# Attention of five batches beside four tiles, x kept in memory between, and the last two tiles' h by seven products

## The chip, the core and the metric

The kernel runs on one core of a Trainium2 chip. TensorE (PE) multiplies matrices into PSUM banks; VectorE (DVE), ScalarE (ACT) and GpSimd (POOL) work on elements; SyncE (SP) issues all DMA transfers from one queue. The metric is the device time of one execution in microseconds, lower is better. Each engine takes its instructions in a fixed order and waits on semaphores for the results of the others.

## The reference

Two parts. Attention on q, k, v of 8 batches, 8 heads, 576 positions, 64 features: scores `q k^T / 8` plus a slope times the distance for each head, masked to the 128 positions that end at the query's own, softmax, times v. Its output, laid out as x of 4608 tokens x 512 features, goes through an MLP:

```python
scores = scale * np.matmul(q, k.transpose(0, 1, 3, 2))
scores = np.where((rel >= 0) & (rel < window), scores + bias[None], -1e9)
attn = softmax(scores)                      # window 128, bias = -slope * |rel|
x = np.matmul(attn, v)                      # as 4608 x 512
h = x @ w_in                                # 512 -> 2048
g = 0.5 * h * (1.0 + erf(h / sqrt(2)))
return g @ w_out                            # 2048 -> 512
```

All inputs and outputs are float32.

## The kernel before

The 4608 tokens are 9 tiles of 512 (tile 0 to 8), which do not match the 8 batches of 576: batch b fills the end of tile b and the start of tile b+1. Products of float32 are made of float16 pairs: each operand is split into a high part (a cast, on ACT or POOL) and a low part, the scaled operand less the high part (`low_part`, L249, on DVE), and three matmuls (high x high, high x low, low x high) add up in PSUM.

A tile of the MLP has two halves. `mlp_in` makes h for one of 16 blocks of 128 features with 12 matmuls of 128x512 (L763); `gelu` takes GELU on ACT (L786), the high part g on POOL (L787) and the low part on DVE. Then `mlp_out` (L809) makes four column blocks of o, each over all 16 blocks of g, 12 matmuls for 4 of these; `put` evicts them (L820 on ACT, L822 on DVE) and sends them out. A tile is a loop of 32 steps: steps 0 to 15 are the blocks of h, steps 16 to 31 a quarter of an o block each.

Attention of a batch is four units of two heads. `scores` (L533) makes them for bands, `biased` (L563, DVE) adds the bias while leaving PSUM, `softmax` takes maxima (L652, DVE) and exponentials (L655, ACT), POOL makes the high weights e_main (L664), `low_weights` the low ones on DVE; SP's transposing DMAs turn e_main to et (L674). `weigh` (L716) multiplies et by v into av, and `leave` writes av as high and low part (L736 and `low_part`) straight into x of the two tiles. `split_qk`, `split_v`, `stat_v` and the scales prepare the next batch's operands.

Tiles 0 and 1 and batches 0 to 2 are placed instruction by instruction by a long string `ORDER`, each name a task that goes one step further. From tile 2 on the code is the loop: beside tile t stand the four units of batch t+1, their scores at the steps `SCORES_AT` and their weighted sums at `WEIGH_AT` of the same tile. The framework puts the resulting instructions on each engine's queue by its own priorities, so the queue's order can differ from the order of the code.

The last two tiles multiply by seven products: a tile is cut in 2x2 blocks, and seven products of half-size blocks of sums of x and of w replace eight. The sums are made on DVE: `sums_of_weights_out` for w_out, `sums_of_weights` for w_in, `sums_of_x` for x (L890 to L940). FAST and FAST_OUT are the first tile whose h and whose out are made that way: 8 and 7. Thus tile 7 makes h by 192 ordinary matmuls and out by 336 of 128x256 (L1098), tile 8 both by 336 of 128x256 (`Seven`, L1011; `seven_all`, `seven_out`). The sums of w_out are made after tile 6's loop and beside tile 7's h, those of w_in beside tile 7's out.

Of the kernel before, what the change touches and what calls it, by code (L numbers as in the profile page):

```python
# [1380 lines left out]
```

## Time and profile before

| | |
|---|---|
| median of 3 runs | 885.36 us (885.20 to 886.47) |
| profiled execution | 885.17 us |
| its span, first to last instruction | 883.4 us |
| PE busy | 871.1 us (99%) |
| DVE busy | 717.3 us (81%) |
| ACT busy | 543.5 us (62%) |
| POOL busy | 197.9 us (22%) |
| granted clock of PE | 1.00 |

The rows below come from that one execution. A group of instructions carries the line of before's code that issues it; `low_part` is a helper, so all low parts share L249 and are told apart by their tiles. A matmul's record is longer than its share of the engine, since matmuls are pipelined: a group's cost on PE is read from start to start.

### The profile page before, as it was taken

The numbers are of one execution on the slowest core, as the hardware profiler recorded it, in microseconds if no ns is written. First come the engines' busy times: TensorE is split into PE (matmuls) and PEld (weight loads), VectorE is DVE, ScalarE is ACT, GpSimd is POOL, SyncE is SP. The second block draws the span as 40 slices with busy tenths as digits, with TensorE's granted clock in tenths as the row PEclk, the third lists the DMA queues.
The fourth block names the chain that finished last, engine by engine and source line by source line (L and its number), as shares of the span: only waits on it lengthen the run. The fifth ranks groups of instructions, "written<-read, shape, count | busy, mean of one in ns | idle before, by whom it ended". The sixth has DMA issues, their size and how long they took to land.

```text
span 883.4 us, 18563 instructions
## 1 busy us (share of the span) xinstructions
PE 871.1 (99%) x7447; PEld 481.5 (55%) x7447; DVE 717.3 (81%) x1385; ACT 543.5 (62%) x1144; POOL 197.9 (22%) x416
## 2 busy tenths in 40 slices
PE   9899999999999999999999999999999999999998
PEld 4644445545454555455455445545545554588887
DVE  7999999999739874888587875888477999998871
ACT  7999969798635662564474454566355357744750
POOL 2100000122015440452125421543054320000000
PEclk9999999999999999999999999999999999999999
DMA  9955666552652236334622454224132230001001
GB/s 308 306 180 207 199 173 138 165 159 56 173 149 55 55 78 185 94 57 85 184 73 55 102 143 134 55 55 108 49 55 56 66 91 1 1 13 37 1 1 48
DMA packets 174598, 91.63 MB, mean 104 GB/s; under 512 B 133680, under 2 KB 156336, under 8 KB 174384
## 3 DMA queue, kind: packets, MB, share of 16 engines
q1 hardware_dynamic: 174512, 90.45, 37.6%
q8 instruction: 58, 0.95, 0.5%
q14 instruction: 28, 0.23, 0.1%
HBM read 46.53 MB, written 9.44 MB: 63 GB/s over the span
## 4 chain that ended last, share of the span: by engine, by line
PE 80%; DVE 11%; ACT 4%; DMA 2%; issue 2%; POOL 0%; SPq 0%; DVEq 0%; ACTq 0%; POOLq 0%
PE h L763 29%; PE o L809 27%; PE av L716 5%; PE sc L533 4%; PE u_out L1098 4%; PE o L806 2%; PE u L1011 2%; PE v L1011 2%; DMA raw<-w_out 1%; DVE s L563 1%; PE z_out L1098 1%; PE y_out L1098 1%; PE v_out L1098 1%; PE x_out L1098 1%; DVE e_main L249 1%
## 5 line engine op out<-in xcount | busy, mean ns | idle before, releaser
L763 PE MATMUL h<-x,wi 128*128 128x512 f16 x1536 | 336.3, 379 | 0.3 <-DVE wi L249 0.2
L763 PEld LDWEIGHTS <-wi 128*128 128x128 f16 x1536 | 148.2, 98 | 178.7 <-DVE wi L249 1.7
L809 PE MATMUL o<-wo,g 128*128 128x512 f16 x864 | 191.7, 379 | 0.0
L809 PEld LDWEIGHTS <-g 128*128 128x128 f16 x1152 | 111.3, 98 | 133.5
L655 ACT ACTIVATE s<-s,nmax 128x192 f32<-128x192 f32 x252 | 111.5, 445 | 36.0 <-DVE nmax L652 35.8
L249 DVE SCALAR_TENSOR_TENSOR e_main<-s,z,e_main 128x192 f16<-128x192 f32 x252 | 119.4, 509 | 11.8 <-POOL e_main L664 11.5
L787 POOL TENSOR_SCALAR g<-g,sg 128x512 f16<-128x512 f32 x96 | 78.8, 829 | 212.9 <-ACT g L786 212.5
L786 ACT ACTIVATE g<-h,gs 128x512 f32<-128x512 f32 x96 | 62.9, 687 | 73.8 <-PE h L763 42.2
L664 POOL TENSOR_SCALAR e_main<-s,z 128x192 f16<-128x192 f32 x180 | 89.8, 518 | 78.6 <-ACT s L655 58.1
L249 DVE SCALAR_TENSOR_TENSOR g<-g,sg,g 128x512 f16<-128x512 f32 x96 | 84.0, 901 | 21.3 <-POOL g L787 21.2
L563 DVE SCALAR_TENSOR_TENSOR s<-sc,cs,bias_h 128x384 f32<-128x384 f32 x112 | 64.3, 609 | 13.5 <-PE sc L533 13.4
L809 PE MATMUL o<-wo_first,g 128*128 128x512 f16 x288 | 66.1, 379 | 0.0
L652 DVE TENSOR_REDUCE nmax<-s 128x5 f32<-128x960 f32 (+1 forms) x56 | 58.1, 1047 | 3.2 <-POOL s L568 2.1
L806 PE MATMUL o<-zo,g 128*128 128x512 f32 x128 | 56.7, 597 | 0.0
L533 PE MATMUL sc<-kbuf,qbuf 64*64 64x192 f16 (+1 forms) x1656 | 53.0, 254 | 3.1 <-DVE s L563 1.8
L568 POOL MEMSET s<- 64x64 f32 (+1 forms) x112 | 19.2, 172 | 158.9 <-DVE s L563 150.7
L736 ACT ACTIVATE x<-av,cx 128x448 f16<-128x448 f32 (+6 forms) x52 | 24.5, 482 | 45.8 <-PE av L716 40.9
L655 ACT ACTIVATION_READ_ACCUMULATOR s<-s,nmax 128x1 f32 x252 | 47.9, 190 | 0.0
L716 PEld LDWEIGHTS <-vbuf 128*64 128x64 f16 x1680 | 40.4, 111 | 8.2 <-issue 6.7
L533 PEld LDWEIGHTS <-qbuf 64*64 64x64 f16 x1512 | 34.3, 106 | 18.4 <-issue 17.5
L716 PE MATMUL av<-et,vbuf 128*64 128x128 f16 (+1 forms) x1680 | 42.7, 210 | 0.3 <-DVE s L563 0.3
L820 ACT ACTIVATE ob<-o,so 128x512 f32<-128x512 f32 x12 | 8.2, 682 | 54.3 <-PE o L809 54.3
(270 smaller groups left out, 1147.3 us busy)
## 6 DMA issues: line engine op xcount, KB each, us to landing
v<-vp SPq DMA_DIRECT2D x32, 320.0 KB, 5.6
out<-ob SPq DMA_DIRECT2D x34, 256.0 KB, 2.3
raw<-w_in SPq DMA_DIRECT2D x8, 1024.0 KB, 11.7
raw<-w_out SPq DMA_DIRECT2D x8, 1024.0 KB, 5.1
q<-qp SPq DMA_DIRECT2D x7, 1152.0 KB, 6.3
k<-kp SPq DMA_DIRECT2D x7, 1152.0 KB, 6.0
qbuf<-qp SPq DMA_DIRECT2D x4, 288.0 KB, 6.1
kbuf<-kp SPq DMA_DIRECT2D x4, 288.0 KB, 5.2
```

The costliest lines, as they stand in the source:

```text
L249: return nc.vector.scalar_tensor_tensor(out=dst, in0=src, scalar=scale, in1=high, op0=ALU.mult, op1=ALU.subtract)
L533: done = nc.tensor.matmul(ps[bank][o, n, 0:W], a, m, start=(i == 0), stop=(i == len(terms) - 1 and b > 0), skip_group_check=True,)
L563: yield nc.vector.scalar_tensor_tensor(out=s[:, bank[0] : bank[0] + k, :], in0=ps[bank][:, 0:k, 0:W], scalar=cs, in1=bias.broadcast_to([P, ...
L655: yield nc.scalar.activation(s[:, i, :], s[:, i, :], AF.Exp, bias=nmax[:, i : i + 1], accum_out=z[:, i : i + 1])
L664: yield nc.gpsimd.tensor_scalar(e[:, i, 0, c], s[:, i], z[:, i : i + 1], 1.0, op0=ALU.mult, op1=ALU.mult)
L716: done = nc.tensor.matmul(av[r, (j - blocks[0]) * QB : (j - blocks[0] + len(js)) * QB], v32s[b][:, hp, kb, r] if b < EXACT else vbuf[:, vi ...
L763: done = nc.tensor.matmul(ph, wi[n][:, a, cc, k * P : (k + 1) * P], x[:, cc, b, :], start=(i == 0), stop=(i == 3 * NCC - 1),)
L786: yield nc.scalar.activation(g32, ph, AF.Gelu, scale=gsc[t, n])
L787: yield nc.gpsimd.tensor_scalar(g[:, r, 0], g32, gsg[t, n], 1.0, op0=ALU.mult, op1=ALU.mult)
L806: done = nc.tensor.matmul(o, g[:, r, c], zo[n][:, n % 2, k * DM : (k + 1) * DM], start=(fc == first), stop=(fc == last))
L809: done = nc.tensor.matmul(o, g[:, r, a, c], wo[n][:, b, k, :], start=(fc == first and i == 0), stop=(fc == last and i == 2),)
L1098: nc.tensor.matmul(ps[name][:, tb], f(d, a)[:, k, tb * P : (tb + 1) * P], w(d, b, k), start=first, stop=True, skip_group_check=True,)
```

## The change

FAST becomes 7, so that tile 7 makes its h by seven products too. For that the sums of w_out and w_in and of tile 7's x must be there when tile 7 starts. Attention of batches 3 to 7 is no longer bound to the tile beside it: its 20 units are placed by two tables over the 128 steps of tiles 2 to 5 (step 0 is the first of tile 2), five batches beside four tiles, and tile 6 has none, but the sums of weights. `split_v(3)` goes into the early string. Since x of a later tile is then ready long before its tile, and there is room for two x only, `leave` writes pieces of x of tiles 4 to 8 into a stage of four slots, SP sends each to memory (36 writes), and `load_x` brings a tile's x back (5 loads of 1 MB). The early string, the PSUM banks and the turns of the buffers are new tables.

```diff
-FAST = 8
+FAST = 7
+LOAD_AT = 29
+SCORES_AT = (2, 8, 14, 19, 29, 34, 40, 44, 53, 59, 65, 69, 79, 84, 90, 94, 104, 110, 115, 118)
+WEIGH_AT = (16, 21, 26, 26, 42, 45, 48, 52, 65, 71, 74, 79, 90, 97, 97, 102, 115, 121, 126, 126)
+SPLIT_AT, STAT_AT, SUMS_AT = (1, 1, 1, 1), (8, 10, 9, 8, 10), (26, 28, 35, 38)
+STAGED = 4
+ATTEND = 5
 FAST_OUT = 7
 HT = TT // 2
 NTILE = NT // TT
...
-z0 z0 b b z0 s0 m00 s0 x00 m00 z1 m00 z1 x00 b F s0 z2 x00 x00 m01 x00 m01 n00 n00 n00 x01 z1 b z2 x01 s1 x01 x01 a0
...
+z0 z0 b b z0 b s0 z1 z1 m00 m00 x00 x00 s0 z1 F x00 m00 b z2 s0 x00 m01 x00 m01 x01 x01 s1 n00 x01 x01 n00 n00 s1 a0
...
+    memory = ctx.enter_context(tc.tile_pool(name="x_all", bufs=1, space=bass.MemoryType.DRAM))
...
+    stage, staged = [], {}
     def x_tile(t):
         if t not in xt:
+            if t >= STAGED:
+                turn_of["x"] = stage[1]
             xt[t] = room([P, NCC, 2, TT], F16, "x", f"x{t}", 2)
         return xt[t]
+    def x_in_memory(t):
+        if t not in staged:
+            staged[t] = memory.tile([P, NCC, 2, TT], F16, name=f"x_all{t}")
+        return staged[t]
+    def place_of_x(t, hp, at, n):
+        if t < STAGED:
+            return x_tile(t)[:, hp, :, at : at + n]
+        if not stage:
+            stage.extend([room([P, 4, 2, TT], F16, "x", "stage", 2), turn_of["x"]])
+        k = stage[2] % 4 if len(stage) > 2 else 0
+        stage[2:] = [k + 1]
+        return stage[0][:, k, :, 0:n]
+    def load_x(t):
+        yield nc.sync.dma_start(x_tile(t), x_in_memory(t))
...
-            x = x_tile(t)[:, hp, :, at : at + n]
-            c = sx[t] if b < EXACT else cx[b, t] if t < B else cx_last
+            x = place_of_x(t, hp, at, n)
+            c = sx[t] if b < EXACT else cx[b, t]
             yield nc.scalar.activation(x[:, 0], av[:, :n], AF.Copy, scale=c)
             yield low_part(x[:, 1], av[:, :n], c, x[:, 0])
+            if t >= STAGED:
+                yield nc.sync.dma_start(x_in_memory(t)[:, hp, :, at : at + n], x)
...
-    def sums_of_x(t, i):
+    def sums_of_x(t, i, places):
 
         x = x_tile(t)[:, 2 * i : 2 * i + 2]
-        r = next_of(pairs).rearrange("p (c n) -> p c n", c=2)
+        r = places[i].rearrange("p (c n) -> p c n", c=2)
...
-    def seven_all(t):
+    def seven_all(t, beside=None):
...
-        for _ in seven_out(t, q[last]):
-            pass
+        for n, _ in enumerate(seven_out(t, q[last])):
+            if beside:
+                beside(n)
...
+        "3V": stat_v(3), "3Q": split_qk(3), "4q": load_qk(4), "3s": split_v(3),
...
-    SCORES_AT, WEIGH_AT = (2, 11, 16, 21), (11, 20, 31, 31)
-    PIECE_AT = (0, 0, 0)
-    PARTS_AT, SUMS_AT = (1,), (9, 12)
-    parts = list(range(NWP // 2))
-    for t in range(2, NTILE):
-        b = t + 1
-        at = {(s + PIECE_AT[i], i): hp for hp, s in enumerate(SCORES_AT) for i in range(3)}
+    def steps(b):
+        return SCORES_AT[(b - 3) * NPAIR : (b - 2) * NPAIR], WEIGH_AT[(b - 3) * NPAIR : (b - 2) * NPAIR]
+    def last_scale():
+        pwx[B] = pwv[B - 1]
+        sx[B] = small([P, 1], f"sx{B}", 3, tag="sx")
+        yield inverse(sx[B], pwx[B], 12)
+        cx_last = small([P, 1], "cxl", 1)
+        cx[B - 1, B] = cx_last
+        yield nc.vector.tensor_scalar(cx_last, pwv[B - 1], sx[B], 2.0 ** -27, op0=ALU.mult, op1=ALU.mult)
+    beside = {}
+    def at(step, *tasks):
+        beside.setdefault(step, []).extend(tasks)
+    def attend(st):
+        for i in range(3):
+            run(scores(st, BANKS[PIECES[i]]))
+            run(biased(st, BANKS[PIECES[i]]))
+        for part in range(2):
+            run(softmax(st, part))
+            run(low_weights(st, part))
+    def gather(st):
+        for part in range(2):
+            run(weigh(st, [part]))
+            run(leave(st, [part]))
+    for b in range(3, B):
+        first, done = steps(b)
+        for hp in range(NPAIR):
+            at(first[hp], lambda st=unit(b, hp): attend(st))
+        if b + 1 < B:
+            at(first[-1] + SPLIT_AT[b - 3], lambda b=b: run(split_qk(b + 1, unit(b, 2).nmax[:, NG - 1 : NG])))
+        if b + 2 < B:
+            at(first[-1] + SPLIT_AT[b - 3] + 2, lambda b=b: run(load_qk(b + 2)))
+        at(steps(b - 1)[1][-1] + 1 if b > 3 else 1, lambda b=b: (b > 3 and run(split_v(b)), b + 1 < B and run(load_v(b + 1))))
+        at(first[0] + STAT_AT[b - 3], lambda b=b: run(stat_v(b + 1, unit(b, 0).nmax[:, NG - 1 : NG]) if b + 1 < B else last_scale()))
+    for b in range(3, B):
+        for hp in range(NPAIR):
+            at(steps(b)[1][hp], lambda st=unit(b, hp): gather(st))
+    for t in range(STAGED, FAST + 1):
+        at(2 * NFC * (t - 3) + (LOAD_AT if t < FAST else NFC), lambda t=t: run(load_x(t)))
+    rests = []
+    base = 2 * NFC * (ATTEND - 2)
+    at(base + SUMS_AT[0], lambda: rests.append(room_for_sums()), lambda: sums_of_weights_out(0, unit(B - 1, 3).z[:, 8 : 8 + 1]))
+    at(base + SUMS_AT[1], lambda: sums_of_weights_out(1))
+    at(base + SUMS_AT[2], lambda: rests.append(room_for_features()), lambda: sums_of_weights_out(2))
+    at(base + SUMS_AT[3], lambda: sums_of_weights_out(3))
+    base += 2 * NFC
+    at(base + NFC, lambda: room_for_halves(*rests))
+    for n in range(NWP // 2):
+        at(base + NFC + 4 * n, lambda n=n: sums_of_weights(n))
+    for n in range(2):
+        at(base + NFC + 8 + 4 * n, lambda n=n: sums_of_x(FAST, n, later[2:4]))
+    def next_x(n):
+        if n == 0:
+            run(load_x(FAST + 1))
+        if n in (3, 4):
+            sums_of_x(FAST + 1, n - 3, later[0:2])
+    for t in range(2, FAST):
         run(tile_scales(t, range(NWP)))
         run(out_scale(t))
-        if t == FAST:
-            seven_all(t)
-            break
-        if t >= FAST_OUT:
-            rest_of_v = room_for_features()
-            for fc in range(NFC):
-                run(mlp_in(t, fc))
-                run(gelu(t, fc))
-                if fc in PARTS_AT:
-                    sums_of_weights_out(parts.pop(0))
-                if fc in SUMS_AT:
-                    sums_of_x(t + 1, SUMS_AT.index(fc))
-            room_for_halves(rest_of_ld, rest_of_v)
-            for n, _ in enumerate(seven_out(t)):
-                if n + 1 < NWP // 2:
-                    sums_of_weights(n)
-                if n == 6:
-                    turns[:] = later[2:4]
-                    sums_of_weights(NWP // 2 - 1)
-            continue
         for step in range(2 * NFC):
             if step < NFC:
                 run(mlp_in(t, step))
                     mlp_out(t, tb, fc)
                 if q == 3:
                     run(put(t, tb))
-            if b >= B:
-                continue
-            for i in range(3):
-                if (step, i) in at:
-                    st = unit(b, at[step, i])
-                    run(scores(st, BANKS[PIECES[i]]))
-                    run(biased(st, BANKS[PIECES[i]]))
-                    if i == 2:
-                        for part in range(2):
-                            run(softmax(st, part))
-                            run(low_weights(st, part))
-            if step == 1:
-                run(split_v(b))
-                if b + 1 < B:
-                    run(load_v(b + 1))
-                    if t > 2:
-                        run(load_qk(b + 1))
-            if step == 6:
-                if b + 1 < B:
-                    run(stat_v(b + 1, unit(b, 0).nmax[:, NG - 1 : NG]))
-                else:
-                    pwx[B] = pwv[B - 1]
-                    sx[B] = small([P, 1], f"sx{B}", 3, tag="sx")
-                    inverse(sx[B], pwx[B], 12)
-                    cx_last = small([P, 1], "cxl", 1)
-                    nc.vector.tensor_scalar(cx_last, pwv[B - 1], sx[B], 2.0 ** -27, op0=ALU.mult, op1=ALU.mult)
-            for hp in range(NPAIR):
-                if WEIGH_AT[hp] == step:
-                    for part in range(2):
-                        run(weigh(unit(b, hp), [part]))
-                        run(leave(unit(b, hp), [part]))
-            if step == SCORES_AT[-1] + 3 and b + 1 < B:
-                run(split_qk(b + 1, unit(b, 2).nmax[:, NG - 1 : NG]))
-        if t + 1 == FAST_OUT:
-            rest_of_ld = room_for_sums()
-            for n in range(3):
-                sums_of_weights_out(parts.pop(0), None if n else unit(b, 2).z[:, 8 : 8 + 1])
+            for task in beside.pop((t - 2) * 2 * NFC + step, ()):
+                task()
+    for t in range(FAST, NTILE):
+        run(tile_scales(t, range(NWP)))
+        run(out_scale(t))
+        seven_all(t, next_x if t == FAST else None)
```

**On DVE in tile 3, before.** The low parts of g for blocks 12 to 15 (`g3_3<-g32_3_12` to `15`; the first number is the tile) with one low part of x (`x5<-av4_0_5`: batch 4, unit 0) and two scales:

```order
L249 SCALAR_TENSOR_TENSOR g3_3_5033<-g32_3_12_5034,sg3_0_4489,g3_3_5033 128x512
L249 SCALAR_TENSOR_TENSOR g3_3_5033<-g32_3_13_5051,sg3_0_4489,g3_3_5033 128x512
L249 SCALAR_TENSOR_TENSOR g3_3_5033<-g32_3_14_5068,sg3_0_4489,g3_3_5033 128x512
L249 SCALAR_TENSOR_TENSOR x5_5017<-av4_0_5_4980,cx4_5_4762,x5_5017 128x320
L751 TENSOR_SCALAR gs5_0_7006<-pww_94,pwx5_4758 128x8
L249 SCALAR_TENSOR_TENSOR g3_3_5033<-g32_3_15_5085,sg3_0_4489,g3_3_5033 128x512
```

**The same place after.** `stage` is the slot that x goes through, `q32_5` and `k32_5` are q and k of batch 5, `s4_3` the scores of batch 4's last unit:

```order
L256 SCALAR_TENSOR_TENSOR stage_3937<-av4_1_4_5310,cx4_4_3659,stage_3937 128x256
L256 SCALAR_TENSOR_TENSOR e_main_108<-s4_3_5180,z4_3_5224,e_main_108 128x192
L256 SCALAR_TENSOR_TENSOR stage_3937<-av4_1_5_5332,cx4_5_4893,stage_3937 128x320
L256 SCALAR_TENSOR_TENSOR e_main_108<-s4_3_5180,z4_3_5224,e_main_108 128x192 x4
L256 SCALAR_TENSOR_TENSOR g3_3_5149<-g32_3_14_5385,sg3_0_4614,g3_3_5149 128x512
L256 SCALAR_TENSOR_TENSOR qbuf_104<-q32_5_4230,scq5_5283,qbuf_104 128x2304
L256 SCALAR_TENSOR_TENSOR kbuf_105<-k32_5_4231,scq5_5283,kbuf_105 128x2304
L783 TENSOR_SCALAR gs5_0_7600<-pww_96,pwx5_4889 128x8
L256 SCALAR_TENSOR_TENSOR stage_3937<-av4_2_4_5423,cx4_4_3659,stage_3937 128x256
L256 SCALAR_TENSOR_TENSOR g3_3_5149<-g32_3_15_5402,sg3_0_4614,g3_3_5149 128x512
```

The splitting of q and k, which stood 46 rows behind block 15 before, now stands ahead of it, and the low weights of batch 4's last unit too.

**On DVE in tile 6, before.** The low parts of g for blocks 12 to 15, then the evictions (`s7_2`) of batch 7's third unit:

```order
L249 SCALAR_TENSOR_TENSOR g6_3_8754<-g32_6_12_8755,sg6_0_8242,g6_3_8754 128x512
L249 SCALAR_TENSOR_TENSOR g6_3_8754<-g32_6_13_8772,sg6_0_8242,g6_3_8754 128x512
L249 SCALAR_TENSOR_TENSOR g6_3_8754<-g32_6_14_8789,sg6_0_8242,g6_3_8754 128x512
L249 SCALAR_TENSOR_TENSOR x8_8738<-av7_0_8_8683,cxl_8479,x8_8738 128x512
L751 TENSOR_SCALAR gs8_0_10231<-pww_94,pwv7_7254 128x8
L249 SCALAR_TENSOR_TENSOR g6_3_8754<-g32_6_15_8806,sg6_0_8242,g6_3_8754 128x512
L752 TENSOR_SCALAR sg8_0_10232<-sww_95,sx8_8477 128x8
L563 SCALAR_TENSOR_TENSOR s7_2_8849<-sc7_2_0_8823,cs7_8024,bias_h_64 128x384
```

**After.** `wi6`, `wi7` are pieces of w_in, `room_s` and `slots` hold sums of them, `room_x` their halves:

```order
L256 SCALAR_TENSOR_TENSOR g6_3_9276<-g32_6_12_9277,sg6_0_9018,g6_3_9276 128x512
L939 TENSOR_TENSOR room_x_9347<-room_s1_9093,room_x_9347 128x512
L935 TENSOR_TENSOR room_s0_9092<-room_s0_9092,room_s1_9093 128x2x256
L939 TENSOR_TENSOR room_x_9347<-room_s1_9093,room_x_9347 128x512
L256 SCALAR_TENSOR_TENSOR g6_3_9276<-g32_6_13_9294,sg6_0_9018,g6_3_9276 128x512
L930 TENSOR_TENSOR room_s1_9093<-wi7_861 128x1024
L939 TENSOR_TENSOR slots2_9096<-room_s0_9092,slots2_9096 128x512
L256 SCALAR_TENSOR_TENSOR g6_3_9276<-g32_6_14_9311,sg6_0_9018,g6_3_9276 128x512
L930 TENSOR_TENSOR room_s0_9092<-wi6_854 128x1024
L783 TENSOR_SCALAR gs8_0_10458<-pww_96,pwv7_7155 128x8
L256 SCALAR_TENSOR_TENSOR g6_3_9276<-g32_6_15_9328,sg6_0_9018,g6_3_9276 128x512
```

The unit of attention is gone from here; sums of w_in, which stood in tile 7 before, are mixed with the low parts of g, and those of w_out stand ahead of them.

**On SP at the end of tile 3, before.** Transposes of batch 4's last unit, loads for batch 6, outputs of tile 3, the first transposes of batch 5:

```order
L674 DMA_TRANSPOSE et4_3_5417<-e_main_106 128x16x128
L467 DMA q32_6_5771<-qp 128x4x576
L468 DMA k32_6_5772<-kp 128x4x576
L823 DMA out_0<-ob3_2_5548 128x512
L823 DMA out_0<-ob3_3_5600 128x512
L419 DMA v32_6_5766<-vp 128x5x128 x4
L674 DMA_TRANSPOSE et5_0_5876<-e_main_106 128x20x128
```

**After.** `x_all4<-stage` writes a piece of tile 4's x to memory, `x4<-x_all4` loads it:

```order
L498 DMA k32_6_5407<-kp 128x4x576
L769 DMA x_all4_3940<-stage_3937 128x2x256
L769 DMA x_all5_5117<-stage_3937 128x2x320
L855 DMA out_0<-ob3_0_5521 128x512
L769 DMA x_all4_3940<-stage_3937 128x2x256
L432 DMA x4_5936<-x_all4_3940 128x4096
L449 DMA v32_6_5720<-vp 128x5x128
L769 DMA x_all5_5117<-stage_3937 128x2x320
L449 DMA v32_6_5720<-vp 128x5x128 x3
L855 DMA out_0<-ob3_1_5749 128x512
```

The loads for batch 6 and the outputs are as before; the writes of x's pieces and the load of tile 4's x now stand between them.

## Rows read from the trace of the kernel before

**Rows 1.** The page, engines (busy us, share, instructions) and PE in 40 slices
```profile
PE 871.1 (99%) x7447; PEld 481.5 (55%) x7447; DVE 717.3 (81%) x1385; ACT 543.5 (62%) x1144; POOL 197.9 (22%) x416
...
PE   9899999999999999999999999999999999999998
```

**Rows 2.** Windows (span, then busy us and instructions of each engine), tiles 3 and 6
```profile
348.50:443.30 94.80, 94.80 (x821) 47.59 (x818) 72.42 (x151) 50.39 (x112) 33.23 (x68) 1.00 0.41 101
...
633.00:728.00 95.00, 95.00 (x845) 47.87 (x842) 78.96 (x140) 47.69 (x117) 37.21 (x68) 1.00 0.28 62
```

**Rows 3.** Windows, h and out of tile 7, then of tile 8
```profile
727.84:769.29 41.45, 41.45 (x199) 18.79 (x193) 38.54 (x58) 29.99 (x45) 0.00 (x0) 1.00 0.00 1
769.29:805.97 36.68, 36.68 (x338) 32.87 (x336) 35.99 (x52) 15.44 (x25) 0.00 (x0) 1.00 0.07 23
805.97:842.70 36.73, 36.73 (x339) 32.92 (x337) 28.78 (x46) 26.29 (x44) 0.00 (x0) 1.00 0.03 9
842.70:883.40 40.70, 36.79 (x338) 32.74 (x335) 17.34 (x27) 12.16 (x19) 0.00 (x0) 1.00 0.08 27
```

**Rows 4.** Waits of PE (total us, times, longest), the largest
```profile
PE tp L634 <- ACT s L606: 2.1, 1, 2.1
```

**Rows 5.** Timeline of PE (start, us, line, operation, tiles), start of tile 8
```profile
805.97 1.47 PE L1011 MATMUL u<-x,wi 128*128 128x256 f16 x12
807.28 1.47 PE L1011 MATMUL v<-x,wi 128*128 128x256 f16 x12
```

**Rows 6.** Groups of DVE (busy us, mean ns | idle before), 348.5 to 443.3 us
```profile
L249 DVE SCALAR_TENSOR_TENSOR e_main<-s,z,e_main 128x192 f16<-128x192 f32 x36 | 18.4, 546 | 2.4 <-POOL e_main L664 2.3
...
L249 DVE SCALAR_TENSOR_TENSOR g<-g,sg,g 128x512 f16<-128x512 f32 x16 | 14.2, 922 | 3.2 <-POOL g L787 3.2
...
L563 DVE SCALAR_TENSOR_TENSOR s<-sc,cs,bias_h 128x384 f32<-128x384 f32 x16 | 9.1, 609 | 3.0 <-PE sc L533 3.0
...
L652 DVE TENSOR_REDUCE nmax<-s 128x5 f32<-128x960 f32 (+1 forms) x8 | 8.3, 1049 | 0.7 <-POOL s L568 0.5
...
L249 DVE SCALAR_TENSOR_TENSOR x<-av,cx,x 128x256 f16<-128x256 f32 (+1 forms) x9 | 4.5, 509 | 1.0 <-ACT x L736 0.9
...
L822 DVE TENSOR_SCALAR ob<-o,so 128x512 f32<-128x512 f32 x2 | 1.5, 740 | 0.0
```

**Rows 7.** Timeline of DVE in tile 3 (last part: idle before, releaser)
```profile
391.08 3.25 DVE L249 SCALAR_TENSOR_TENSOR e_main<-s,z,e_main 128x192 f16<-128x192 f32 x6
...
398.14 0.74 DVE L249 SCALAR_TENSOR_TENSOR g<-g,sg,g 128x512 f16<-128x512 f32 x1
...
418.80 0.67 DVE L219 COPY quarters<-stq 32x2 f32<-32x2 f32 x4
...
426.79 2.61 DVE L249 SCALAR_TENSOR_TENSOR qbuf<-q,scq,qbuf 128x2304 f16<-128x2304 f32 x1
```

**Rows 8.** Timeline of PE in tile 3
```profile
397.04 1.43 PE L533 MATMUL sc<-kbuf,qbuf 64*64 64x192 f16 x54
...
398.40 7.94 PE L809 MATMUL o<-wo,g 128*128 128x512 f16 x36
...
408.87 1.55 PE L716 MATMUL av<-et,vbuf 128*64 128x128 f16 x54
```

**Rows 9.** Timeline of DVE, sums of weights in tile 7
```profile
799.12 1.22 DVE L898 TENSOR_TENSOR slots<-wi 128x1024 f32<-128x1024 f16 x1
800.26 0.68 DVE L901 TENSOR_TENSOR room_s<-room_s 128x512 f32<-128x512 f32 x1
```

**Rows 10.** DMA issues (count, KB each, median us to landing)
```profile
out<-ob SPq DMA_DIRECT2D x34, 256.0 KB, 2.3
...
raw<-w_out SPq DMA_DIRECT2D x8, 1024.0 KB, 5.1
...
et<-e_main SPq DMA_TRANSPOSE x56, 4.1
```

**Rows 11.** Durations in ns (min/median/max) of low parts of g on DVE
```profile
L249 DVE SCALAR_TENSOR_TENSOR g<-g,sg,g x96: 708/749/1181, 168.7 to 683.0; 128x512 f16<-128x512 f32 x96
```

More of the change, by code (lines that the diff above doesn't have):

```diff
@@ new lines @@
+B2 M10 A5 S2 M10 S2 B2 M10 A7 B2 N01 M20 M20 J5 S3 B2 M11 M20 M11 M11 N10 o M11 M11 J5 N10 O M20 M10 M10 N11 lQ M11
+N10 v1 N10 zs N11 N11 N10 N11 M20 M20 B2 lV J7 B3 v1 J7 O B2 tl zs o M21 o S3 zs S3 v2 J7 o M21 v2 q2 p2 B3 v2 B3 zs
+1c tl M20 v2 B3 B3 M21 v2 v2 q2 o M20 M21 v2 M30 v2 o zs o M21 v2 B3 v2 B3 zs q2 v2 q2 B3 v2 q2 B3 v2 O N10 M30 M31 k1
+y0 N11 M20 M21 M20 v2 M31 M20 N20 N20 M20 v2 k1 M20 M21 N20 N20 v1 v2 Y0 q2 v2 O N20 M30 M30 q2 O M21 M30 zs q2 y1 q2
+M21 M30 1c v2 p3 M21 zs N21 M21 q2 Y1 N21 x0 q2 M30 O zs N21 x1 p1 v2 q2 X0 M30 X1 q2 x0 h0 N20 O N21 M31 q2 q2 M31 k0
@@ new lines @@
+1g5 2M11 3V 2M00 1H12 2B0 2M11 2M11 2M10 2M10 1H15 3V 2M00 2M00 1H8 2M01 2M00 1g4 1H11 2M01 3V p0 2M11 2M01 2M01 1H10
+2M01 3V 1H12 2N00 2M00 1H8 1g5 1g6 1H7 1H7 1H10 1H10 1g8 2M10 1H11 2N00 1H7 1H11 3V 1H15 2N00 1g1 1H9 2N00 1H12 3V
+2N00 1g6 3V 1g1 1H15 h3 2M01 1g6 1g7 1H9 2M01 h3 1g10 2M10 3V 2M01 1g7 1g8 3q 2M11 1g7 2M11 1H14 h3 2M01 2N01 2N00 1g8
+2N01 1H12 1g9 2M01 1s 1g10 2M10 1g9 2N01 1H11 1H14 1g9 1H15 1H13 2N10 1g11 2M01 1g10 1H13 2M10 2M10 2N01 2S2 1g12 2B2
+2B2 2B2 2B2 2S2 2S2 3V 1H14 1H14 1H13 2B2 2B2 1g11 1g15 3Q 1g11 3V h3 2M20 3V 1H13 2N01 1o0 1o0 2B2 2N10 2B2 1g13 2S3
@@ new lines @@
+2M20 3V 1g13 2M11 2B2 3Q 2N10 3Q 2N11 2M11 2M21 2M20 2S3 1g12 2M10 3Q 2M20 2M11 2N11 2N10 2N11 2M20 2M11 2N11 2M20
+2M10 3V 2N10 2M21 2M21 2M21 2S3 3Q 3V 2B3 3Q 2B3 2M20 3Q 3V 2B3 1o3 1g15 3V 2N10 2M20 1g12 1o0 3Q 2B3 2M21 2B3 2B3 1o2
+2B3 3Q 2M21 1g14 1g13 2M30 2M30 3Q 2N11 1o1 3Q 3Q 2B3 1o2 2y0 2M20 3V 2M20 2M30 2M30 2M21 2y1 2M30 2M30 2M20 2M20 3Q
+2Y1 2N20 2M20 2B3 2M31 2N20 3Q 2M21 2M31 2M21 3Q 3V 3V 1g15 2M21 2N20 2M31 1g14 3Q 2Y0 2M30 2M31 1o2 2M21 2X1 3Q 2N20
+2M31 1g14 3Q 2N20 2N21 1o2 2M31 2M30 2N21 2N21 2M31 2N20 1o0 2x1 2X0 2N21 3Q 2N21 2M30 1o1 1o1 2M30 2X0 2M31 3Q 2N30
@@ L94 @@
+1o1 2M31 1k2 1k2 2X1 2x0 2M30 2M31 2x1 1o3 2M30 1k0 2N31 4q 1o3 1o3 2y2 2N30 2M31 2N31 2x0 2N30 2M30 3Q 2N31 3V 2N31
+2N30 2Y2 2N30 3Q 1k3 1k0 2N31 1k1 2N30 2x2 2y3 2X2 2Y3 2x3 2x3 2X3 4q 2x2 1k3 2X2 1k1 2X3 3s 3s
 """
 PSUM_BANKS = (
-    "0075146217345260217346506321340574256301035624013540276041252134263017254017450721271427112471540612"
-    "753130512573062573604312574023160521752216542"
+    "0541235016743201576230541054716502305712701374602142116573012604175163421040214636314613412462136047"
+    "563537645036714037162702451313256043206757341"
@@ L100 @@
     "s": "1010101011001",
-    "ob": "01211202102120210001022120",
+    "ob": "01010112010220121012010201",
     "x": "11001010",
-    "nmax": "010101100101",
-    "z": "010101010101",
-    "g": "0213320101230",
-    "ld": "01010101010",
-    "stv": "0010",
+    "nmax": "010110011010",
+    "z": "010101011010",
+    "g": "3201102303210",
+    "ld": "01010100101",
+    "stv": "1000",
+    "wo": "201301230123",
     "pwv": "1020",
-    "scv": "2121",
-    "wo": "031201230123",
-    "gs2": "1230",
-    "sg2": "0210",
+    "scv": "2112",
+    "gs2": "3130",
+    "sg2": "2200",
     "stq": "111",
-    "pwq": "100",
+    "pwq": "010",
     "scq": "111",
-    "pwx": "001",
     "cs": "110",
-    "sx": "210",
-    "cx": "02132",
-    "gs8": "1",
+    "pwx": "101",
+    "sx": "212",
+    "gs8": "0",
     "sg8": "0",
-    "so": "11",
+    "cx": "05251",
+    "so": "00",
 }
```

57 lines of the change are left out of this document (19 added, 38 removed).

## The prediction

> **What bounds the kernel now.** I read the page's first part: TensorE (PE) is busy for 871.1 of 883.4 us, VectorE (DVE) for 81% [rows 1]. In the digits every slice of PE after the first two is a 9, so the sum of PE's work sets the time, and other engines matter only where they make PE wait. Next the stretches: from 253.5 us on, PE is busy for all of each tile's stretch (two of the five are shown: 94.80 of 94.80, 95.00 of 95.00), at a granted clock of 1.00, which is the upper of its two levels, and DVE for 72.42 and 78.96 us of these [rows 2]. So DVE has some 22 us to spare in a tile of 95. The last two tiles look the same, up to the final 40.70 us, where PE does 36.79 and the last output leaves (3.9 us) [rows 3]. Of PE's 12.3 us of idle time (883.4 less 871.1) these 3.9 are the tail, and the other 8.4 lie ahead of the second tile's end; the largest single wait there is that of a transpose for ScalarE's (ACT) exponentials, 2.1 [rows 4].
>
> **The change part by part.** The profiled execution took 885.17 us (span 883.4 and 1.77 around it), the median of the runs is 885.36, so the sum is made against 885.17 and 0.2 is added.
>
> *PE, tile 7.* h by the ordinary way is 192 matmuls of 128x512, from 727.84 to 769.29: 41.45 us, 0.216 each [rows 3]. By seven products it is 4 column groups x 7 x 12 = 336 matmuls of 128x256. Tile 8 does just these: 12 start at 805.97 and the next 12 at 807.28, 0.109 each [rows 5], so 336 take 36.6. The difference is 41.45 - 36.6 = 4.85 us less. All other matmuls stay as many as they were; on PE attention is only moved. If nothing else happened, 885.36 - 4.85 = 880.5.
>
> *What pays for it on DVE.* The attention of five batches now stands beside four tiles (2 to 5). A tile of attention-free work is 384 matmuls, 384 x 0.216 = 82.9 us of PE; a stretch of 94.9 thus holds 12.0 us of attention for four units, so five units make 82.9 + 15.0 = 97.9. DVE's 72.42 [rows 2] holds 14.2 for the low parts of g and 1.5 for output evictions (L822) [rows 6]; the remaining 56.7 grow by 5/4 to 70.9, in all 86.6 of 97.9: 88%, against 76% before. Still less than PE on average, so what counts is a place where PE needs something that stands behind a crowd in DVE's in-order queue.
>
> *First place, tile 3.* The first column block of o needs the low part of g for block 15. Before, that low part starts at 398.14 and the o block that reads it (fourth group of twelve, 0.216 x 12 = 2.6 each, of the 36 that start at 398.40) begins near 403.6 [rows 7, 8]: about 5 us of lead, the splitting of the next batch's q (2.61, and as much for k behind it) coming only at 426.79. After, the two splits stand directly ahead of it. From the eviction of the scores at step 40 to that low part, DVE's rows are 8 evictions of 384 columns and 2 of 192, 4 maxima, 8 low parts of g, 18 low weights, 5 low parts of x, the two splits, the scale's chain (2.9 from the row at 418.80 to the last of its thirteen) and small ones (2.4). By busy time over count in rows 6 and 7: 8 x 0.57 + 4 x 1.04 + 8 x 0.89 + 18 x 0.51 + 5 x 0.50 + 5.2 + 2.9 + 2.4 = 37.9; records overlap (the 35 groups of that stretch, the costliest of them shown, add up to some 76.6 where 72.4 is busy), so x 0.945 = 35.8. PE has in the same time 11 steps x 2.59 = 28.5, three sets of weighted sums (1.55) and one of scores (the other half of a unit's 3.0, 1.45) [rows 8]: 34.6. DVE is late by 1.2, and each of the two units adds a bubble on POOL's products (2.3 for four units [rows 6]) or ACT's sums unless a low part of g fills it. Bounds: 0 (if records overlap more) and 4; I take 2.0.
>
> *Second place, tile 6.* All sums of w_out and most of those of w_in now come before the low part of the last block of tile 6; before, the sums of w_in were made in tile 7. From the first output of tile 5 to that low part the order counts 16 sums of 128x1024 at 1.14 (start to start) to 1.22 and 56 of 128x512 at 0.60 to 0.68 [rows 9], 18 to 20 and 34 to 38, and beside them 16 low parts of g, 18 of weights, and evictions and maxima of two units, by the rates of the first place some 36 us: 88 to 94 together. PE has 12 + 16 + 3 steps there, two sets of scores and four of weighted sums: 31 x 2.59 + 2 x 1.45 + 4 x 1.55 = 89.4. Bounds: 0 and 4.6; the lower end is nearer, since most of this stretch has no work of attention on POOL beside it and runs at start-to-start rates: 0.5.
>
> *Attention's own chain.* From scores to weighted sums the shortest distance falls from 9 steps to 7. Before, the last low weights of such a 9-step unit end at 394.3 and its weighted sums start at 408.87 [rows 7, 8]; less 4.1 for the transposing transfer [rows 10], 10.4 us are spare, and two steps cost 5.2. It stays hidden: 0. If it didn't, the wait would be of the order of a transfer, 4.1.
>
> *x by way of memory.* SyncE's queue gets 36 writes and 5 loads more, each transfer between instructions that it already held, transposes among them. A write waits for DVE's low part of x and holds up what is behind it; the transposes there belong to the next unit, whose weights DVE makes later, so they lose nothing. Writes are below the 256 KB that take 2.3 us, a load is 1 MB like the w_out pieces, 5.1 [rows 10]. Loads are issued some 11 steps (28 us) ahead of the first matmul that reads them, the last one beside tile 7's 36.7 us of out [rows 3]. Cost 0; without that cover 2.3 + 5.1 = 7.4 for one load.
>
> *Tile 7 and 8 on DVE.* Seven products in tile 8 cost DVE 28.78 and 17.34 us of PE's 36.7 each; tile 7 gets the same, and the 38.5 and 36.0 us of before, swollen by weight sums, go [rows 3]. PE saw no gap in either. 0, and nothing to gain.
>
> *Beginning.* The new order leaves DVE's milestones within a few us of where they were, in both directions; PE's 8.4 us of idle time bound the gain, the 2.1 of its largest wait is the size of a likely loss. I take 0, with -4 to +2.
>
> Sum: -4.85 + 2.0 + 0.5 = -2.35, so 885.36 - 2.35 = 883.0.
>
> A rule that speaks against this change: here the low part of g (both inputs in SBUF) takes 0.708 to 1.181 us, median 0.749, while POOL works beside it [rows 11], so records of one shape stretch by up to 0.43. The Trainium skill (SBUF — State Buffer, Terms) says that VectorE and GpSimd take turns on a port pair which is locked for a whole instruction, the loser blocking fully. The spread agrees with that. By that rule attention drawn together makes more such meetings and every low part of g goes towards its longest, which is the 4.6 us a tile of rival D below; by the rows' means nothing is added to the 0.89 that the sum has.
>
> **Rivals.** *A, no new wait:* the low parts come in time, 880.5. For it: the average of 88% leaves 11 us a tile. Against: the queue's order at the first place. *C, the gain is eaten:* both places cost their upper bounds or the beginning loses 2: stalls of 3.5 to 6.5, 884 to 887, say 885.4. For it: DVE's bubbles on POOL, 2.3 and 3.2 a tile [rows 6], grow with the units. *D, slower: DVE becomes the bound in the crowded tiles.* Place: tiles 3 to 5, where five units and their splits meet 16 low parts. Price: the fullest tile holds 95 us of DVE by these rates (86.6 and a second pair of splits, 5.2, with its scale's chain, 2.9), bubbles of five units at 0.9 add 4.5, and 16 low parts of g at the longest record, 1.18 for a mean of 0.89 [rows 6, 11], add 4.6: 104 against 98 for PE, 5 to 6 in that tile; a tile at the average is at 86.6 + 9.1 = 95.7 and loses nothing, the first place then loses 4 and the second 1: 880.5 + 10.5 = 891. It decides from the point where DVE's share of a tile passes 95%. *E, that x comes late:* a load stands behind a write that waits, 7.4 for one tile, 880.5 + 2.5 + 7.4 = 890.4; against it, the 28 us of lead. *That the change doesn't do what it says* I rule out: the order shows 336 matmuls in place of 192.
>
> **How the numbers follow.** What a measurement of this kernel can tell from no change is about 0.2%, 1.8 us: faster is below 883.6, slower above 887.1. My forecast (waits of 1 to 4 us, 881.5 to 884.5) 0.38, of which 0.28 lies below 883.6; A 0.24 (with a better beginning down to 878); C 0.17, nearly all of it within 0.2% (0.02 above 887.1); D 0.16, E 0.05. Faster 0.28 + 0.24 = 0.52; same 0.10 + 0.15 = 0.25, slower 0.02 + 0.21 = 0.23. The range leaves out a better beginning beyond 878.5 and the worst of D and E: 878.5 to 890.5.
>
> **What would show it.** Right: the stretch of tile 7's h takes 36.6 and matmuls are 109 ns apart; PE's waits name DVE's low part of g (o <- g) for 1 to 4 us, in tile 3 above all; DVE's share of tiles 3 to 5 rises to 85 to 95%; no wait names the loads of x. A is right if PE is solid from tile 2 to the end. D shows as waits of h on ACT or of scores on DVE, several us in tiles 4 and 5. I would be wrong if PE waited for x or for weights by the transposes, or if the beginning moved by over 3 us.

## The result and the profile after

The changed kernel takes 892.12 us (median of 4 runs, 891.37 to 892.47) where the kernel before took 885.83 beside it: ratio 1.0069, interval 1.0056 to 1.0081. It is 6.3 us slower; 883.0 had been forecast, with 878.5 to 890.5 as the range. The profiled execution took 892.47 us.

The page after, its engines, PE in 40 slices and the granted clock:

```profile
PE 872.1 (98%) x7591; PEld 497.8 (56%) x7591; DVE 728.3 (82%) x1409; ACT 536.4 (60%) x1148; POOL 225.2 (25%) x416
...
PE   9899999999999999998999999999999899999998
...
PEclk9899999999999999999999999999999999999999
```

Against [rows 1], POOL is busy for 27 us more with the same 416 instructions, and PE, with 4.85 us less to do, for 1.0 more. PE's idle time is 890.6 - 872.1 = 18.5 us where it was 12.3; the slices with an 8 are at tile 3 and tile 6. Who PE waited for (total us, times, longest):

```profile
PE tp L664 <- ACT s L636: 3.3, 2, 2.9
PE o L841 <- POOL g L819: 3.1, 2, 2.3
PE h L795 <- ACT g L818: 2.9, 4, 1.5
PE o L841 <- DVE g L256: 1.7, 2, 1.1
```

The first is the old wait of the start, longer than in [rows 4]; the other three are new. The windows of tile 6 after (655 to 710 us, busy us of PE, PEld, DVE, ACT, POOL, then clock), and three short ones in its worst place:

```profile
655.00:710.00 55.00, 50.56 (x225) 21.89 (x223) 52.16 (x72) 24.63 (x40) 29.18 (x16) 0.97 0.10 35
...
706.00:708.00 2.00, 1.05 (x3) 0.44 (x4) 2.00 (x6) 0.47 (x1) 0.00 (x0) 0.71 0.00 0
708.00:710.00 2.00, 2.00 (x6) 0.70 (x5) 2.00 (x4) 1.26 (x3) 0.00 (x0) 0.50 0.00 0
710.00:712.00 2.00, 2.00 (x10) 0.85 (x9) 2.00 (x3) 0.13 (x1) 0.00 (x0) 0.93 0.00 0
```

PE's rows there, with the idle time before each and its releaser:

```profile
703.81 0.60 PE L841 MATMUL o<-wo,g 128*128 128x512 f16 x2 [0.80 <-POOL g L819]
705.02 0.82 PE L841 MATMUL o<-wo,g 128*128 128x512 f16 x3 [0.60 <-DVE g L256]
706.95 0.61 PE L841 MATMUL o<-wo,g 128*128 128x512 f16 x1 [1.11 <-DVE g L256]
```

PE loses 4.4 us in the 55 by waiting, and after three waits within five microseconds its clock is granted at the lower of its two levels (0.50, 1.2 GHz) for some 3 us, which costs about 1.7. POOL's 16 instructions, the high parts of g, take 29.18 us: 1.82 each, where the median of all 96 such records is 0.78. Durations of these records (min/median/max in ns), before and after:

```profile
L787 POOL TENSOR_SCALAR g<-g,sg x96: 687/784/1733, 167.3 to 680.9; 128x512 f16<-128x512 f32 x96
L819 POOL TENSOR_SCALAR g<-g,sg x96: 683/783/4538, 172.1 to 703.7; 128x512 f16<-128x512 f32 x96
```

The pieces of POOL in the chain of waits of that stretch (660 to 712 us), and DVE's instructions beside the third of them:

```profile
659.62 2.03 POOL g L819
665.38 3.44 POOL g L819
680.40 4.12 POOL g L819
688.65 3.42 POOL g L819
701.61 2.16 POOL g L819
```

```profile
680.25 0.68 DVE L934 TENSOR_TENSOR room<-room 128x512 f32<-128x512 f32 x1
680.85 0.68 DVE L939 TENSOR_TENSOR wi<-room_s,wi 128x512 f16<-128x512 f32 x1
...
683.26 0.68 DVE L939 TENSOR_TENSOR room_x<-room_s,room_x 128x512 f16<-128x512 f32 x1
684.54 1.17 DVE L256 SCALAR_TENSOR_TENSOR g<-g,sg,g 128x512 f16<-128x512 f32 x1 [0.59 <-POOL g L819]
```

POOL's g stands in the chain five times, for 15 of 52 us, though it is a short instruction, 0.78 at the median. DVE works back to back beside it, on sums and low parts that read two operands from SBUF. POOL's record of 680.40 lasts through six of them and ends only after DVE has stopped, at its low part, to wait for that very high part. All five records of the chain end so, after two to six instructions of DVE; DVE's five pauses for POOL add up to 2.8 us.

In tile 3 the same thing stands in three rows, of DVE, POOL and PE (the last with its idle time and releaser):

```profile
409.12 2.60 DVE L256 SCALAR_TENSOR_TENSOR qbuf<-q,scq,qbuf 128x2304 f16<-128x2304 f32 x1
411.65 2.60 DVE L256 SCALAR_TENSOR_TENSOR kbuf<-k,scq,kbuf 128x2304 f16<-128x2304 f32 x1
...
415.06 0.73 DVE L256 SCALAR_TENSOR_TENSOR g<-g,sg,g 128x512 f16<-128x512 f32 x1
```

```profile
406.89 0.78 POOL L819 TENSOR_SCALAR g<-g,sg 128x512 f16<-128x512 f32 x1
410.20 4.54 POOL L819 TENSOR_SCALAR g<-g,sg 128x512 f16<-128x512 f32 x1 [2.52 <-ACT g L818]
```

```profile
414.79 0.61 PE L841 MATMUL o<-wo,g 128*128 128x512 f16 x2 [2.26 <-POOL g L819]
```

POOL's high part of block 15 begins at 410.20 and ends at 414.74, right after DVE's second split; the same instruction took 0.78 before it. This is the place that the prediction named, but it had the low part late; here the high part is late first, on POOL.

What was forecast of tile 7's h and of x came as said. PE's timeline at its start shows 12 matmuls every 1.31 us, as [rows 5], and the loads of x land in 4.9 us at the median, with no wait of PE named after them:

```profile
739.87 1.47 PE L1043 MATMUL u<-x,wi 128*128 128x256 f16 x12
741.18 1.47 PE L1043 MATMUL v<-x,wi 128*128 128x256 f16 x12
...
x<-x_all SPq DMA_DIRECT2D x5, 1024.0 KB, 4.9
```

### The profile page after: what moved, and what is told of

Same layout as the page of the kernel before. It is cut to its first block, busy times and chain, and to the rows that moved or that the text cites. A ratio compares the mean times of both kernels' runs of the same rounds, so it can differ in the third digit from the quotient of the medians.

```text
span 890.6 us, 19044 instructions
## 1 busy us (share of the span) xinstructions
PE 872.1 (98%) x7591; PEld 497.8 (56%) x7591; DVE 728.3 (82%) x1409; ACT 536.4 (60%) x1148; POOL 225.2 (25%) x416
## 5 line engine op out<-in xcount | busy, mean ns | idle before, releaser
L795 PE MATMUL h<-x,wi 128*128 128x512 f16 x1344 | 296.4, 379 | 3.1 <-ACT g L818 2.9
L795 PEld LDWEIGHTS <-wi 128*128 128x128 f16 x1344 | 129.5, 98 | 159.2 <-issue 5.6
L841 PEld LDWEIGHTS <-g 128*128 128x128 f16 x1152 | 111.3, 98 | 140.5 <-POOL g L819 4.0
L819 POOL TENSOR_SCALAR g<-g,sg 128x512 f16<-128x512 f32 x96 | 107.1, 1122 | 148.7 <-ACT g L818 145.5
L256 DVE SCALAR_TENSOR_TENSOR e_main<-s,z,e_main 128x192 f16<-128x192 f32 x252 | 115.9, 497 | 11.4 <-POOL e_main L694 10.9
L694 POOL TENSOR_SCALAR e_main<-s,z 128x192 f16<-128x192 f32 x180 | 87.0, 501 | 77.3 <-ACT s L685 51.8
L598 POOL MEMSET s<- 64x128 f32 (+1 forms) x112 | 19.1, 171 | 183.5 <-DVE s L593 176.3
L1043 PEld LDWEIGHTS <-wi 128*128 128x128 f16 x384 | 37.6, 98 | 4.6
L1131 PEld LDWEIGHTS <-g 128*128 128x128 f16 x384 | 37.6, 98 | 4.3
```

The source lines that it names most:

```text
L256: return nc.vector.scalar_tensor_tensor(out=dst, in0=src, scalar=scale, in1=high, op0=ALU.mult, op1=ALU.subtract)
L694: yield nc.gpsimd.tensor_scalar(e[:, i, 0, c], s[:, i], z[:, i : i + 1], 1.0, op0=ALU.mult, op1=ALU.mult)
L795: done = nc.tensor.matmul(ph, wi[n][:, a, cc, k * P : (k + 1) * P], x[:, cc, b, :], start=(i == 0), stop=(i == 3 * NCC - 1),)
L819: yield nc.gpsimd.tensor_scalar(g[:, r, 0], g32, gsg[t, n], 1.0, op0=ALU.mult, op1=ALU.mult)
L841: done = nc.tensor.matmul(o, g[:, r, a, c], wo[n][:, b, k, :], start=(fc == first and i == 0), stop=(fc == last and i == 2),)
L1043: nc.tensor.matmul(ps[:, k * HT : (k + 1) * HT], w(a, i)[:, k * P : (k + 1) * P], m(b, i),  start=first and n == 0, stop=True, skip_group_ ...
```

## The experiments

Theory L: DVE instructions with two operands in SBUF lock POOL out, and the high part of g comes late. Theory Q, the prediction's: DVE's queue is too full, and the low part comes late. Theory E: the new start costs time. The kernel before was measured again beside each of three groups of these runs (885.58, 885.9 and 885.8 us). The run micro is not in the table, since it computes no attention and no MLP.

| run | median us | ratio to before, 95% interval |
|---|---|---|
| hi6 | 885.05 | 0.9993 (0.9984 to 1.0002) |
| hi3 | 890.10 | 1.0051 (1.0037 to 1.0065) |
| early | 893.54 | 1.0092 (1.0077 to 1.0107) |
| hi6_early | 887.81 | 1.0021 (1.0012 to 1.0029) |
| hiall | 884.81 | 0.9990 (0.9981 to 0.9999) |
| gate3 | 886.26 | 1.0005 (0.9997 to 1.0014) |
| gate3all | 885.03 | 0.9995 (0.9986 to 1.0004) |
| before_hiall | 885.61 | 0.9999 (0.9990 to 1.0008) |
| gate_only | 888.15 | 1.0021 (1.0012 to 1.0031) |
| gate_55_68 | 884.19 | 0.9981 (0.9971 to 0.9990) |

**hi6: tile 6's high parts on ACT.**

```diff
-        yield nc.gpsimd.tensor_scalar(g[:, r, 0], g32, gsg[t, n], 1.0, op0=ALU.mult, op1=ALU.mult)
+        if t == 6:
+            yield nc.scalar.activation(g[:, r, 0], g32, AF.Copy, scale=gsg[t, n])
+        else:
+            yield nc.gpsimd.tensor_scalar(g[:, r, 0], g32, gsg[t, n], 1.0, op0=ALU.mult, op1=ALU.mult)
```

> The high part of g of tile 6 is written by ScalarE instead of GpSimd; VectorE's work stays the same. Theory L (VectorE's sums, which read two SBUF operands back to back, keep GpSimd from writing the high part of g; tile 6's o and h wait for that): the waits of tile 6 (4.5 us of idle PE and 1.4 us at the lower clock) go, 892.1 - 5.9 = 886.2. Theory Q (the forecast's: VectorE's queue is too full in tile 6, low parts come late): the low parts come as late as before, 891 to 892.

Measured 885.05: 7.1 us off. The same stretch in this run, to be held against the row above:

```profile
655.00:710.00 55.00, 55.00 (x256) 24.95 (x255) 54.61 (x85) 35.99 (x58) 0.00 (x0) 1.00 0.11 39
```

PE waits for nothing, and DVE is fuller than before the edit: 54.61 of 55 us, with 85 instructions where there were 72. The whole of tile 6, from its first matmul of h to tile 7's, in the changed kernel and in hi6:

```profile
649.93:739.87 89.94, 85.50 (x385) 37.73 (x384) 67.83 (x97) 30.75 (x49) 29.18 (x16) 0.98 0.09 31
649.82:732.70 82.88, 82.88 (x385) 37.55 (x384) 62.91 (x97) 40.82 (x65) 0.00 (x0) 1.00 0.10 33
```

The same 385 matmuls take 7.1 us less, and DVE's same 97 instructions are busy for 4.9 us less. A full DVE queue alone is thus not what cost the time; Q falls for tile 6 and L stands. The low part of g got shorter too, 0.76 us on average for 0.92. The edit takes away both sides of the meeting at once, POOL's late high parts and DVE's own longer records and pauses; what each of them is worth was not separated.

**hi3: one block of tile 3.** The same edit with `if t == 3 and fc == 15`.

> Only block 15 of tile 3 has its high part of g written by ScalarE. Theory L alone: the wait of 2.3 us of o for GpSimd goes, 889.8. Theory Q alone: the wait is VectorE's queue, nothing changes, 892.1. Both: the high part comes early, but the low part still ends behind the two splits, so that the wait of o changes its releaser to VectorE and shrinks by 0.5 to 1: 891.3.

Measured 890.10, 2.0 less than the changed kernel. PE's wait at that place in the profile:

```profile
414.48 0.39 PE L844 MATMUL o<-wo,g 128*128 128x512 f16 x1 [1.27 <-DVE g L256]
```

The releaser is now the low part of g behind the two splits: in tile 3 both theories hold, POOL's lock for about 1 us and DVE's queue for 1.3. That the median fell by twice what the one wait shrank is in part a matter of the clock: the four runs of hi3 whose mean clock is 0.996 average 890.7 us, three such runs of the changed kernel 891.9. The other two of hi3 have 0.998. This profile also shows a wait of 1.85 us for DVE in tile 4 that the changed kernel's did not have.

**early and hi6_early: the old start.** Order table, banks and turns from the kernel before; the splitting of batch 3's v returns to step 1 of tile 2.

```diff
-    turn_of.update(cs=0, cx=2, g=0, gs2=0, gs8=1, ...)
+    turn_of.update(cs=0, cx=4, g=0, gs2=3, gs8=0, ...)
...
-at(steps(b - 1)[1][-1] + 1 if b > 3 else 1, lambda b=b: (b > 3 and run(split_v(b)), ...))
+at(steps(b - 1)[1][-1] + 1 if b > 3 else 1, lambda b=b: (run(split_v(b)), ...))
```

> The part before the loop (order table, PSUM banks, turns) is the one of the kernel before, all else is as after. Theory E (the new order's wait of 2.9 us at 22.6 us is followed by the lower clock until 31, and the start costs 2.3 more than before): 889.8, and the granted clock is 1.00 in the first 50 us. If the start costs nothing: 892.1.

> Both edits together. Theories L and E: 892.1 - 5.9 - 2.3 = 883.9, faster than the kernel before. Theory Q with E: 889 to 890. If neither: 892.

893.54 and 887.81: with the old start the kernel is 1.4 and 2.8 us slower, not faster. The profile of early shows where 1.4 of it lies: a wait in tile 2, 0.68 in the changed kernel, where the split of v now meets the g of its first blocks:

```profile
282.72 17.39 PE L795 MATMUL h<-x,wi 128*128 128x512 f16 x72 [2.11 <-ACT g L818]
```

That wait came with the edit, so the medians alone don't settle what the start costs. The place of tile 2's first matmul of h does, in the kernel before, the changed kernel and early:

```profile
253.55 2.75 PE L763 MATMUL h<-x,wi 128*128 128x512 f16 x12
254.18 2.12 PE L795 MATMUL h<-x,wi 128*128 128x512 f16 x9
254.31 1.89 PE L795 MATMUL h<-x,wi 128*128 128x512 f16 x8
```

With either start the changed kernel comes to tile 2 at the same time, within 0.2 us, and 0.6 to 0.8 later than the kernel before. The lower clock is no fault of the new start alone either. Windows of 24 to 32 us, of the changed kernel and of hi6_early with the old start:

```profile
24.00:32.00 8.00, 6.47 (x38) 5.20 (x42) 7.61 (x16) 6.29 (x24) 0.39 (x1) 0.57 1.07 338
```

```profile
24.00:32.00 8.00, 6.00 (x57) 5.16 (x56) 7.72 (x22) 7.66 (x29) 0.75 (x2) 0.79 1.08 323
```

Both fall to the lower level after the wait of the first transposes (2.9 and 2.0 us), the new start for longer; the kernel before's profiled execution had 1.00 there, but most of its other runs have a mean clock of 0.996 to 0.999. E falls as the cause of the loss, but for 0.6 us.

**micro: the lock by itself.** Eight POOL instructions as in `gelu`, beside DVE work of one kind at a time.

```python
for k, work in enumerate((alone, splits, maxima, sums, evictions, low_parts, alone)):
    s = pool_work(k)                 # both engines start together
    work()                           # 5 or 20 instructions of one kind on DVE
    for _ in range(8):
        nc.gpsimd.tensor_scalar(g, g32, s, 1.0, op0=ALU.mult, op1=ALU.mult)
```

> Leaves the whole computation out: eight GpSimd instructions of the kind that writes the high part of g (128x512, float16 from float32), six times: alone, beside 5 low parts of 128x2304 (both inputs in SBUF), beside 5 maxima of 128x2304 (one input), beside 20 sums of 128x512 (both in SBUF), beside 20 low parts whose first input lies in PSUM, beside 20 low parts of 128x512 with both in SBUF; then alone again. Theory L (it is the second SBUF input that locks GpSimd out): about 0.7 us each when alone, beside maxima and beside the PSUM form; 2 to 5 us beside the 128x2304 low parts, 1.2 to 2.5 beside sums and 128x512 low parts. Rival R (any busy VectorE slows GpSimd): all stretched alike.

The timeline of POOL for the first six, in that order, eight instructions a row:

```profile
10.07 6.21 POOL L119 TENSOR_SCALAR g<-g,s 128x512 f16<-128x512 f32 x8 [9.63 <-DVE s L86]
16.57 17.21 POOL L119 TENSOR_SCALAR g<-g,s 128x512 f16<-128x512 f32 x8 [0.28 <-DVE s L86]
34.06 6.21 POOL L119 TENSOR_SCALAR g<-g,s 128x512 f16<-128x512 f32 x8 [0.28 <-DVE s L86]
46.93 8.74 POOL L119 TENSOR_SCALAR g<-g,s 128x512 f16<-128x512 f32 x8 [6.66 <-DVE s L86]
64.36 6.21 POOL L119 TENSOR_SCALAR g<-g,s 128x512 f16<-128x512 f32 x8 [8.69 <-DVE s L86]
80.02 8.88 POOL L119 TENSOR_SCALAR g<-g,s 128x512 f16<-128x512 f32 x8 [9.44 <-DVE s L86]
```

6.21 alone, 6.21 beside maxima (one input) and beside low parts whose first input lies in PSUM: no disturbance at all. 8.74 and 8.88 beside sums and low parts of 128x512 with both inputs in SBUF, 17.21 beside the long low parts, where five of the eight POOL records are about as long as the DVE instruction that they meet, 2.87 to 2.99. The seventh piece, alone again, took 6.21. R falls; L has its price. Here it is one DVE instruction for each POOL instruction; in the kernel it is more, two in tile 3 and up to six in tile 6, when the next ones of DVE take the ports first. What decides who comes next is not shown. The rows differ in one thing: in micro each DVE record starts after the one before it has ended (eight of 1.06 us in 8.74), in the kernel before that (0.60 apart for records of 0.68).

**hiall, gate3, gate3all: the rest of the way.** hiall has the edit of hi6 for all of tiles 2 to 6. gate3 has it for tile 6, and holds the splits of batch 5 until block 15 of tile 3 has left PSUM; gate3all has both.

```diff
-SCORES_AT = (..., 40, 44, 53, 59, ...)
+SCORES_AT = (..., 40, 44, 56, 61, ...)
-SPLIT_AT, ... = (1, 1, 1, 1), ...
+SPLIT_AT, ... = (1, 4, 1, 1), ...
-run(split_qk(b + 1, unit(b, 2).nmax[:, NG - 1 : NG]))
+run(split_qk(b + 1, g32_of[3, 15][:, 0:1] if b == 4 else unit(b, 2).nmax[:, NG - 1 : NG]))
```

> The high part of g is written by ScalarE in all of tiles 2 to 6. Theory L with a rest of VectorE's queue in tile 3: against the variant with tile 6 alone (885.1) the 0.7 of tile 2 and about 1 of the 2.5 of tile 3 go: 883.4. If the wait of tile 3 were GpSimd's alone: 882. If ScalarE's extra 0.7 a block delays the exponentials of attention: 886 or more, with waits on ScalarE.

> Tile 6's high parts on ScalarE, and the splits of batch 5's q and k held until block 15 of tile 3 has left PSUM, so that they stand behind its low part; the first two units of batch 5 start three and two steps later. If the two splits ahead of block 15 are what tile 3 waits for, on both engines: 885.1 - 2.5 = 882.6. If something else is late there, the wait stays: 885.

> Both: high parts on ScalarE in tiles 2 to 6 and the splits behind block 15 of tile 3. Only the start's waits are left, so PE's sum alone sets the time: 880.5 + 1 for the lower clock in the start = 881.5, 0.5% faster than the kernel before.

884.81, 886.26 and 885.03, each 1.4 to 3.7 us above what was expected; only hiall is clear of the kernel before, by 0.1%. In hiall the wait of tile 2 is gone and that of tile 3 is 1.42 us for ACT's high part; a wait of 1.14 us came in tile 4, for a GELU behind the high parts of q and k, 2.21 us each on ACT. In gate3 and gate3all tile 3's wait of 2.3 us is gone, and its like stands at the first weighted sums of batch 5, of which this is gate3's:

```profile
456.53 1.24 PE L746 MATMUL av<-et,vbuf 128*64 128x64 f16 x48 [2.52 <-DVE s L593]
```

**before_hiall: the control.** The kernel before with hiall's edit.

> The kernel before with the high part of g written by ScalarE in tiles 2 to 6. Theory L: GpSimd made PE wait nowhere in the kernel before, so nothing is gained: 885.6, within 0.2%. If ScalarE were simply the better engine for this work wherever it stands, it would gain as in the changed kernel: 880.

885.61, ratio 0.9999: nothing gained. Longer records of DVE and POOL were there before (up to 1.18 us in [rows 11], 1.73 on POOL), but no wait of PE names POOL in that kernel.

**gate_only and gate_55_68: which steps batch 5 needs.** gate_only is gate3all with the old steps; gate_55_68 puts batch 5's first two units at 55 and 60 for scores and 68 and 72 for weighted sums.

> High parts on ScalarE in tiles 2 to 6, splits of batch 5 held behind block 15 of tile 3, all steps as in the changed kernel. If the wait of 2.2 us at the first weighted sums of batch 5 came from its scores being put off by three steps, it goes: 885.0 - 2.2 - 1 for the lower clock behind it = 882; if from the splits being late, it stays or becomes a wait of the scores: 885.

> The same with the first two units of batch 5 one or two steps later for scores, and one to three for weighted sums, so that their chain has as many steps as before. Tiles 2 to 6 without waits of over 0.5: 882.5, unless the later sums push what is behind them.

gate_only: 888.15, above both values that were expected; the scores now wait for the splits (2.84 us, for kbuf, in its profile, which is of an execution of 886.14), so the splits have no free place between block 15 and step 53. gate_55_68: 884.19, faster than the kernel before by 0.19%, the fastest of all, but 1.7 above what was expected; tiles 2 and 3 are free of waits and tiles 4 and 5 keep 2.4 us of them. Whether the sums of weights could be mixed so that POOL gets in between was not tried.

## Why the prediction was wrong

*PE's sum, -4.85.* Right: matmuls of 109 ns, 12 in 1.31 us. From tile 7's first matmul of h to the end it is 150.7 us (739.87 to 890.6), where it was 155.6 (727.84 to 883.4).

*Second place, tile 6, 0.5.* This is the step that failed: "the lower end is nearer, since most of this stretch has no work of attention on POOL beside it". I counted DVE's time against PE's and left POOL's own work in that stretch out, the 16 high parts of g. They were the ones locked out. The term is 7.1 us by hi6's median and by tile 6's stretch, of which the profile shows 4.4 as waiting and some 1.7 as lower clock; its upper bound had been 4.6. With the high parts away from POOL, in hi6, PE waits for nothing in tile 6 and the stretch takes 82.88 us, the 82.9 forecast for a tile without attention, so DVE's own time was no obstacle there.

*First place, tile 3, 2.0.* Place and size were near, 2.3 at the wait and 2.7 with a short one beside it; the reason was half right. hi3 shows about 1 us of POOL's lock and then 1.27 of DVE's queue, for which the sum had 1.2 (its terms add up to 38.0, not 37.9). That the whole came near 2.0 is in part luck.

*The rule that speaks against the change.* The Trainium skill (SBUF — State Buffer, Terms) says that the loser of the shared ports blocks fully. I read this off DVE's records alone, and gave it 4.6 us a tile in D's crowded tiles of attention. The direction agrees with every run here (17.21 and 8.74 us beside two SBUF operands for 6.21 alone), but the victim that mattered was POOL and the place tile 6. The longest POOL record of such a part in the kernel before, 1.73 us for a median of 0.78, would have pointed to it; I quoted only DVE's. One thing differs from the rule: in micro POOL's records beside the sums follow each other every 1.09 us, less than a sum (0.69) and a POOL record alone (0.70) together, so DVE is not held for the whole of POOL's record.

*Rival D* had the side and, by luck, nearly the time (891), by another place. DVE's shares of tiles 3 to 5 are 85, 88 and 89% (84.23 of 99.61, 87.76 of 99.49 and 88.58 of 99.39 us), as forecast, and tiles 4 and 5 show no wait at all, so DVE never became the bound that D priced.

*Beginning, 0.* Its size was about right and its parts were not foreseen: in the first 260 us PE waits 6.8 us where it waited 8.4, and loses some 2.7 to the lower clock, of which the kernel before has a share in most runs. The old start makes the changed kernel no faster, and tile 2 begins 0.6 us later than before.

*Chain of attention, x by way of memory, tiles 7 and 8: 0.* Right. The writes of x's pieces took 1.6 to 4.4 us to land, some of them longer than the 2.3 that they were put below, and no wait of PE followed.

Together: 880.5 + 7.1 (tile 6) + 2.7 (tile 3) + 0.7 (a wait of h in tile 2 for ACT's GELU, gone in hiall) = 891.0 of 892.1. Of the last 1.1, 0.6 is the start, where tile 2 begins at 254.18 instead of 253.55; and the kernel before itself took 885.83 beside the changed one, 0.5 more than the 885.36 from which the 880.5 was made.
